# Selective attention and a routed feed-forward layer: the second expert unit's first layer as seven block products

## Chip, core and metric

The kernel runs on one core of a Trainium2 chip. The metric is the time of one execution in microseconds (us), as the device reports it. The engines are TensorE (PE in the profile, with its weight loads as PEld), VectorE (DVE), ScalarE (ACT), GpSimd (POOL) and SyncE (SP, whose queue issues most transfers).

## What is computed

Eight batches of 576 tokens pass an attention layer of 8 heads of 64, whose scores carry a bias from the cumulated `s`. Its output, 512 wide, goes into a feed-forward layer with 8 experts of width 1024, one expert for each token. All is 32-bit.

```python
# attention: x[b, s, :] = softmax(scores + min(bias, 0)) @ v, heads side by side
logits = einsum('bsd,de->bse', x, w_gate)
local_gate = sigmoid(einsum('bsd,de->bse', x, w_local))
for b in range(B):
    prev_e = -1
    for s in range(S):
        fresh_e = argmax(logits[b, s])
        e = fresh_e if s == 0 or local_gate[b, s] < 0.5 else prev_e
        prev_e = e
        p = softmax(logits[b, s])
        h = maximum(x[b, s] @ w1[e], 0)       # 512 -> 1024
        out[b, s] = p[e] * (h @ w2[e])        # 1024 -> 512
```

## The kernel before

The first 202 us are the attention. As batches become ready, the router reads off each token's expert ("codes"), ranks the tokens of an expert, and GpSimd stores their rows into a table in DRAM that is sorted by expert (`scatter`, L371). The last batch's codes and ranks come after the attention (`last_codes`, `late_rows`).

The experts then work through 17 units. A unit is a number of rows of one expert; the letters of `ORDER` say which kind: P and D are 256 rows, X is wider, M and T are made of smaller pieces. Which expert a unit has is only known at run time: `assign_early` places the first five units, `assign_doubles` the other whole units, and both are many tiny VectorE operations. They are generators; the three `yield`s of a whole-unit assignment are in `assign`.

A unit has two layers: phase (1, u) multiplies the turned rows xT by w1, with an activation (relu), phase (2, u) multiplies hT by w2. The phases go (1, 0), (1, 1), (2, 0), (1, 2), (2, 1), (1, 3), ... A layer is done in one of two ways:

- Plain (`layer1`): 8 groups of 4 products over 256 rows, each followed by a relu on ScalarE (L865, L867). A 32-bit product takes two passes through TensorE in the trace, so these are 64.
- Split (`layer_split`): the operands are cut into 2 x 2 blocks, a11 to a22 of the rows and b11 to b22 of the weights, and seven block products do for eight. They need sums of rows, s1 and s2 (`row_sums`, L704 to L706, and `row_fourth`, L710), and sums of weights, t1 and t2 and two in place (`weight_first` to `weight_fourth`, all recorded at L655). Product 6 takes s2 and t2, product 7 b12 after the third sum, product 4 b21 after the fourth. VectorE adds the products up (L763).

`SPLIT = ("DX", "PDX")` says which kinds are split: the first layer of D and X, the second of P, D and X. Sums of weights run on VectorE. Sums of rows run on VectorE in the first layers of the first five units (`adder`), else on GpSimd.

The engines work in the order in which the program issues their instructions. Within a phase, `at(i)` is called after each group or product, and runs what was put there: `plan(layer, unit, i, f)` and `job` (the same, with `i` held to the last step of that phase) hang functions to these places. At each step one pending store of table rows may go too (`self.puts`), held behind that step's ScalarE instruction, and further rows are fetched (`fetch`, L606, into xq, turned by `turn_x`, L641).

Of the kernel before, what the change touches and what calls it, by code (L numbers as in the profile page):

```python
# [63 lines left out]
WIDE, WIDE_MIN = DOUBLE + REST, DOUBLE + REST_MIN  # L64
EARLY = (4, 1)
PIECES = {"P": (DOUBLE,), "D": (DOUBLE,), "X": (WIDE,), "M": (HALF, HALF), "T": (HALF, QUARTER, QUARTER)}
ORDER = "PPDDDDDDDDXTXDMXD"
SPLIT = ("DX", "PDX")
LOOK, REST_FROM, REST_AT = 5, 8, (3, 4)
UNITS_OF = {size: sum(PIECES[u].count(size) for u in ORDER) for size in (DOUBLE, WIDE, HALF, QUARTER)}  # L70
SUM_MIN, SUM_MAX, ONE_MAX, END_MAX = 1e-19, 1e25, 1e12, 1e29
# [446 lines left out]
class Experts:  # L518
    def __init__(self, ctx, tc, w1, w2, out, table, router):
# [17 lines left out]
        loads = 0  # L537
        for kind in ORDER:
            at = []
# [354 lines left out]
    def run(self, recs, wend, out_of):  # L894
        tc, ctx, nc, router = self.tc, self.ctx, self.nc, self.router
# [71 lines left out]
        def plan(what, u, i, *fs):  # L967
            todo.setdefault((what, u, i), []).extend(fs)
# [2 lines left out]
        plan(1, 0, 2, last_codes)  # L971
        plan(1, 1, 1, lambda: loads(0))
        plan(1, 1, 2, late_rows)
        plan(1, 1, 5, lambda: list(router.assign_doubles()))
        rest = router.assign_rest()
        ranges = in_range(ctx, tc, recs, wend, router, out_of, self.bank, router.ones)
        plan(1, end - 1, 3, lambda: next(ranges))
# [10 lines left out]
        def job(what, u, i, f, *args):  # L988

            plan(what, u, i if i == "pre" else min(i, steps[self.kind(u)][what - 1] - 1), lambda: f(*args))  # L990

        for u in range(end):
            if u >= 2:
                job(2, u - 2, "pre" if u > 2 else 1, turn_x, u)
            for layer in range(2):
                if not self.split(u, layer):
                    continue
                if layer:
                    places = (2, u - 1, 5), (1, u + 1, "pre"), (1, u + 1, 2)
                    if u == 0:  # L1000
                        places = (1, 1, 6), (1, 1, 7), (1, 1, 7)
                    elif u == 1:
                        places = (2, 0, 5), (1, 2, 1), (1, 2, 3)
                    elif self.kind(u - 1) == "T":
                        places = (1, u + 1, 6), (1, u + 1, 6), (2, u, "pre")
                    place = (1, u + 1, int(self.deep(u) > 1)) if u + 1 < end else (2, u - 1, 0)
                    if u < 2:
                        place = ((1, 1, "pre"), (2, 0, 2))[u]
                    job(*place, self.row_sums, u, 1)
                else:  # L1010
                    places = (1, u - 1, 5), (2, u - 2, "pre"), (2, u - 2, 2)
                    if self.kind(u - 1) == "T":
                        places = (2, u - 2, 5), (2, u - 2, 6), (1, u, 0)
                    elif self.kind(u - 2) == "T":
                        places = ((2, u - 2, "pre"),) * 3
                    elif u == 2:
                        places = (2, 0, 4), (2, 0, 5), (1, 2, 0)
                    job(2, u - 2, 1 if self.kind(u - 2) in "DX" else "pre" if u > 2 else 3, self.row_sums, u, 0)
                for f, place in zip((self.weight_first, self.weight_second, self.weight_third), places):
                    job(*(place if place[1] < end else (2, u, "pre")), f, u, layer)  # L1020
            if self.kind(u) in "MT":
                for r, place in enumerate(((2, u - 1, 1), (2, u - 1, 3), (1, u + 1, 2), (1, u + 1, 3))):
                    job(*place, self.turn_h, u, r)
# [999 lines left out]
```

## Time and profile before

| | |
|---|---|
| three runs | 677.79, 679.24 (median), 680.12 us |
| profiled execution | 680.58 us, of it 678.8 in the span |
| TensorE, VectorE busy | 98%, 73% of the span |
| GpSimd, ScalarE busy | 54%, 29% of the span |
| granted clock of TensorE | 0.996 |
| unit 0 first layer begins | 202.5 us |
| unit 0 second layer begins | 232.2 us |

All times of the profile count from the start of the span, and the medians of the runs are of whole executions, so a sum over the span is to be put on the profiled execution's own time. A row of the timeline has the start in us, the time that the group of equal instructions took in us, the engine, the line, the operation, output<-inputs, shapes and how many; brackets at its end give the idle time of the engine just before it and what ended it. Tiles are named as in the program: w1b and w2b are weights, wt the sums t1 and t2 of them, xTs and hT the turned operands, xSs and hSs their sums, p the products in PSUM, sa and sb partial results.

### The profile page before, as it was taken

Reading aid. Unit: us, or ns where it says so; the run is one execution under the profiler, and the core shown is the slowest. Engines: PE = TensorE matmul, PEld = TensorE weight load, DVE = VectorE, ACT = ScalarE, POOL = GpSimd, SP = SyncE. Lnnn points to the kernel's source line nnn. Section 1 sums busy time; section 2 is a strip of 40 time slices with the busy share of each in tenths; the row PEclk is TensorE's granted clock in tenths of the full one; section 3 lists DMA queues with packets and bytes.
Section 4 is the critical chain, followed back from the end, with each engine's and each line's share of the span. In section 5 each row is a group of like instructions: output and inputs, shape, how many; then the busy total and the mean of one; then the engine's idle time right before and its main releaser. Section 6 shows DMA issues by size and latency. Waiting matters only on the chain.

```text
span 678.8 us, 18449 instructions
## 1 busy us (share of the span) xinstructions
PE 662.1 (98%) x7501; PEld 571.4 (84%) x7501; DVE 492.5 (73%) x942; ACT 195.3 (29%) x353; POOL 369.6 (54%) x525
## 2 busy tenths in 40 slices
PE   8999999999999999999999999999999999999995
PEld 7888877877788899999999999999589687796884
DVE  4665856886867799878988988955467664766843
ACT  4555635535522212212122122212211111111111
POOL 3562476776744888964555557540642542714733
PEclk9999999999999999999999999999999999999998
DMA  8665665766659798579977565616949796943002
GB/s 263 193 183 158 197 219 151 215 214 210 197 133 392 240 327 288 191 255 364 344 274 231 204 187 186 241 55 235 354 66 386 271 361 132 295 148 112 28 14 76
DMA packets 56549, 145.75 MB, mean 215 GB/s; under 512 B 13104, under 2 KB 33968, under 8 KB 51464
## 3 DMA queue, kind: packets, MB, share of 16 engines
q1 hardware_dynamic: 47352, 124.23, 55.8%
q0 software_dynamic: 9008, 20.11, 8.2%
q8 instruction: 61, 1.00, 0.6%
q14 instruction: 32, 0.26, 0.1%
q10 hardware_dynamic: 96, 0.15, 0.1%
HBM read 123.83 MB, written 20.85 MB: 213 GB/s over the span
## 4 chain that ended last, share of the span: by engine, by line
PE 86%; DVE 6%; issue 4%; POOL 2%; ACT 0%; POOLq 0%; DVEq 0%
PE p L731 26%; PE p L738 25%; PE ps L1218 11%; PE po L1275 6%; PE pb L1275 6%; PE hp L865 3%; PE yp L888 2%; PE hp L856 2%; PE lp L238 1%; PE ph L1236 1%; POOL out_dram L840 1%; DVE wt L655 1%; PE po L1288 1%; DVE w2b L655 1%; PE warm L1142 1%
## 5 line engine op out<-in xcount | busy, mean ns | idle before, releaser
L738 PE MATMUL p<-w2b,hT 128*128 128x256 f32 (+1 forms) x720 | 163.0, 379 | 0.0
L738 PEld LDWEIGHTS p<-w2b,hT 128*128 128x128 f32 (+1 forms) x720 | 133.3, 187 | 21.9 <-PE hp L856 1.6
L731 PE MATMUL p<-xTs,w1b 128*128 128x128 f32 (+1 forms) x1040 | 142.9, 295 | 0.0
L731 PEld LDWEIGHTS p<-xTs,w1b 128*128 128x128 f32 x1040 | 137.9, 191 | 3.6 <-issue 1.6
L1219 ACT ACTIVATE e<-ps 128x768 f32<-128x768 f32 (+1 forms) x96 | 76.4, 885 | 64.1 <-PE ps L1218 58.1
L840 POOL DMA_INDIRECT out_dram<-y,gi x37 | 46.9, 1269 | 74.2 <-ACT y L767 66.3
L767 ACT ACTIVATE y<-y,gi 128x256 f32<-128x256 f32 (+1 forms) x71 | 34.5, 505 | 161.6 <-DVE y L763 161.6
L771 ACT ACTIVATE hT<-hT 128x512 f32<-128x512 f32 (+1 forms) x52 | 36.8, 711 | 143.7 <-DVE hT L763 143.7
L1218 PE MATMUL ps<-qb,kb 64*128 64x384 f32 (+4 forms) x516 | 77.5, 446 | 0.2 <-ACT e L1219 0.2
L1218 PEld LDWEIGHTS ps<-qb,kb 64*128 64x128 f32 x516 | 47.7, 189 | 27.5 <-ACT e L1219 10.3
L371 POOL DMA_INDIRECT table<-xb,idx x54 | 57.3, 1062 | 15.8 <-issue 14.4
L738 PE MATMUL p<-wt,hSs 128*128 128x256 f32 (+1 forms) x272 | 63.3, 379 | 0.0
L710 POOL TENSOR_TENSOR hT<-hT,hSs 128x512 f32<-128x512 f32 (+1 forms) x14 | 21.1, 1508 | 76.8 <-PE p L738 76.8
L731 PE MATMUL p<-xSs,wt 128*128 128x128 f32 (+1 forms) x416 | 58.9, 295 | 0.5 <-DVE wt L655 0.5
L738 PEld LDWEIGHTS p<-wt,hSs 128*128 128x128 f32 (+1 forms) x272 | 50.7, 186 | 8.0
L1202 POOL TENSOR_SCALAR_AFFINE_SELECT e<-e 128x128 f32<-128x128 f32 (+1 forms) x96 | 35.7, 394 | 38.5 <-ACT e L1219 38.2
L731 PEld LDWEIGHTS p<-xSs,wt 128*128 128x128 f32 x416 | 55.6, 192 | 1.2 <-PE p L731 0.7
L763 DVE TENSOR_TENSOR hT<-p,sa 128x512 f32<-128x512 f32 (+1 forms) x48 | 31.2, 666 | 32.7 <-PE p L731 32.7
L1275 PE MATMUL pb<-vg,e 128*64 128x66 f32 x1280 | 41.9, 223 | 4.7 <-issue 4.7
L1275 PEld LDWEIGHTS pb<-vg,e 128*64 128x64 f32 x1280 | 39.7, 138 | 5.6 <-issue 5.4
L1275 PE MATMUL po<-vg,e 128*64 128x66 f32 x1280 | 41.6, 223 | 1.6 <-issue 1.6
L1275 PEld LDWEIGHTS po<-vg,e 128*64 128x64 f32 x1280 | 39.0, 138 | 3.2 <-issue 2.1
(304 smaller groups left out, 951.9 us busy)
## 6 DMA issues: line engine op xcount, KB each, us to landing
w2b<-in_w_dram SPq DMA_DIRECT2D x20, 2048.0 KB, 13.5
w1b<-in_w_dram SPq DMA_DIRECT2D x19, 2048.0 KB, 10.5
va<-in_v_dram SPq DMA_DIRECT2D x32, 320.0 KB, 3.4
xq<-table SPq DMA_DIRECT2D x72, 130.0 KB, 3.7
kb<-in_k_dram SPq DMA_DIRECT2D x31, 288.0 KB, 4.2
qb<-in_q_dram SPq DMA_DIRECT2D x31, 288.0 KB, 3.3
w1b<-in_w_dram SPq DMA_DIRECT2D x4, 512.0 KB
table<-xb,idx POOLq DMA_INDIRECT x54, 5.1
```

The source lines that it names most:

```text
L371: put = self.nc.gpsimd.indirect_dma_start(out=self.halves, in_=src, element_offset=0, in_offset=None, out_offset=bass.IndirectOffsetOnAxis ...
L710: self.adder(u, layer).tensor_tensor(a12, a12, (self.xS, self.hS)[layer][u][1], op=Alu.subtract)
L731: mm(ps[:, m * h : m * h + h], lhsT=b[:, k, (c * of + m) * P : (c * of + m) * P + P], rhs=a[:, k, :], start=m == 0 and k == 0, stop=m == o ...
L738: mm(ps[:p, c * w : c * w + w], lhsT=a[:, k, c * p : c * p + p], rhs=b[:, k, :], start=c == 0 and k == 0, stop=c == parts - 1 and k == n - 1)
L763: nc.vector.tensor_tensor(to[:, c], part, s[:, c], op=Alu.add)
L767: ins = nc.scalar.mul(to[:, c], to[:, c], gi[:p, parts * r + c, 1:2]).ins
L771: return gated(to, r) if layer else nc.scalar.activation(to, to, Act.Relu).ins
L840: put = nc.gpsimd.indirect_dma_start(out=out, out_offset=bass.IndirectOffsetOnAxis(ap=idx, axis=0), in_=y, element_offset=0, bounds_check= ...
L1202: nc.gpsimd.affine_select(out=ap, in_=ap, compare_op=Alu.is_ge, fill=0.0, base=base, pattern=n, channel_multiplier=-1)
L1218: mm(ps[:, h, at : at + z - a], lhsT=kb[d, key : key + P], rhs=qb[d, a:z], start=True, stop=True)
L1219: exps[n, u] = nc.scalar.activation(e[:, :, : WIDTH[u]], ps, Act.Exp, scale=scale).ins
L1275: of = mm(po[part][d, j - a, :], lhsT=weights_of(n, c, j, h), rhs=vgs[n % NV][:, c if j < 2 * G1 else G1 + c, h, :], start=(first and i == ...
```

## The change

Unit 1 becomes a D, so its first layer is split as well. Its row sums are put at step 3 of phase (1, 0), and its sums of weights at steps 4, 5 and 6, which is behind the last rows' codes on VectorE. The assignment of whole units, until now run in one go at step 5 of phase (1, 1), is taken up at five places, (1, 1, 5), (2, 0, 1), (2, 0, 3), (1, 2, 1) and (1, 2, 3); with three `yield`s it has four pieces, and the fifth call finds nothing left.

```diff
-ORDER = "PPDDDDDDDDXTXDMXD"
+ORDER = "PDDDDDDDDDXTXDMXD"
...
-        plan(1, 1, 5, lambda: list(router.assign_doubles()))
+        doubles = router.assign_doubles()
+        for place in ((1, 1, 5), (2, 0, 1), (2, 0, 3), (1, 2, 1), (1, 2, 3)):
+            plan(*place, lambda: next(doubles, None))
...
-                    job(2, u - 2, 1 if self.kind(u - 2) in "DX" else "pre" if u > 2 else 3, self.row_sums, u, 0)
+                    elif u == 1:
+                        places = (1, 0, 4), (1, 0, 5), (1, 0, 6)
+                    if u == 1:
+                        job(1, 0, 3, self.row_sums, u, 0)
+                    else:
+                        job(2, u - 2, 1 if self.kind(u - 2) in "DX" else "pre" if u > 2 else 3, self.row_sums, u, 0)
```

On VectorE, behind the last operation of the last rows' codes (L315), before the change come the last rows' ranks:

```order
L315 SCALAR_TENSOR_TENSOR incl<-seg,hot 128x152
L332 TENSOR_TENSOR at<-pos,base 128x144
L334 TENSOR_TENSOR base<-base,pos 128x8
L335 TENSOR_TENSOR at<-at,hot 128x144
L337 TENSOR_REDUCE row<-at 128x18
```

and after it unit 1's sums of rows and weights, with two additions behind its products:

```order
L315 SCALAR_TENSOR_TENSOR incl<-seg,hot 128x152
L704 TENSOR_TENSOR xSs<-xTs 128x256
L705 TENSOR_TENSOR xSs<-xSs,xTs 128x256
L706 TENSOR_TENSOR xTs<-xTs 128x2x128
L655 TENSOR_TENSOR wt_4100<-w1b 128x1024
L655 TENSOR_TENSOR wt_4100<-w1b,wt_4100 128x1024
L655 TENSOR_TENSOR w1b<-w1b 128x2x512
L763 TENSOR_TENSOR hT<-p_4167,sa 128x4x128
L655 TENSOR_TENSOR w1b<-w1b,wt_4100 128x2x512
L710 TENSOR_TENSOR xTs<-xTs,xSs 128x2x128
L763 TENSOR_TENSOR sb<-p_4187,sa 128x512
L332 TENSOR_TENSOR at<-pos,base 128x144
```

Ten operations now stand between the codes and the ranks, whose stores into the table wait for them.

On VectorE, before unit 0's sums of weights for its second layer (wt from w2b), the rest of the assignment stood in one piece:

```order
L413 TENSOR_SCALAR bof<-be 128x7
L416 TENSOR_SCALAR bstep<-n_f 128x8
L418 TENSOR_TENSOR bstep<-bstep,start 128x8
L419 TENSOR_TENSOR bstep<-bstep,start 128x7
L420 TENSOR_TENSOR bpast<-bpast,bstep 128x56
L423 TENSOR_REDUCE br<-bpast 128x7
L424 SCALAR_TENSOR_TENSOR br<-lane,br 128x7
L426 TENSOR_SCALAR bof<-br,start 128x7
L433 TENSOR_TENSOR bused<-n_f,bend 128x8
L434 TENSOR_SCALAR bused<-bused 128x8
L435 TENSOR_TENSOR bused<-bused,n_f 128x8
L466 TENSOR_TENSOR a0used<-a0used,bused 128x8
```

and now only its first piece does:

```order
L413 TENSOR_SCALAR bof<-be 128x7
L763 TENSOR_TENSOR hT<-p_4289,sb 128x4x128
L655 TENSOR_TENSOR wt_4300<-w2b 128x1024
L655 TENSOR_TENSOR wt_4300<-w2b,wt_4300 128x1024
L655 TENSOR_TENSOR w2b<-w2b 128x4x256
L763 TENSOR_TENSOR y<-p_4321,sa 128x256
L655 TENSOR_TENSOR w2b<-w2b,wt_4300 128x4x256
L416 TENSOR_SCALAR bstep<-n_f 128x8
```

The pieces from L416 and from L423 stand behind unit 0's sums now, and the one from L433 behind unit 2's second sum of weights.

On TensorE unit 1's 20 remaining plain products behind the ranks' (L323, L324) become four block products, with three ahead of them; before:

```order
L238 MATMUL lp<-xt_3689,wx 32x96 x32
L865 MATMUL hp<-xTs,w1b 128x256 x32
L323 MATMUL pos<-incl,first 128x152
L324 MATMUL pos<-hot,later 128x152
L865 MATMUL hp<-xTs,w1b 128x256 x20
```

and after:

```order
L865 MATMUL hp<-xTs,w1b 128x256 x20
L731 MATMUL p_4154<-xTs,w1b 128x128 x8
L731 MATMUL p_4167<-xTs,w1b 128x128 x8
L731 MATMUL p_4187<-xSs,wt_4100 128x128 x8
L323 MATMUL pos<-incl,first 128x152
L324 MATMUL pos<-hot,later 128x152
L731 MATMUL p_4226<-xTs,w1b 128x128 x8
L731 MATMUL p_4239<-xSs,wt_4100 128x128 x8
L731 MATMUL p_4253<-xTs,w1b 128x128 x8
L731 MATMUL p_4289<-xTs,w1b 128x128 x8
```

The third block product (p6, from xSs and wt) needs VectorE's sums, and the ranks' products stand behind it. In the other places that the text speaks of, GpSimd has one table store less in unit 1's first phase and one more behind, and unit 3's row sums move to step 1 of phase (2, 1), since unit 1 is now a D.

## The prediction

> **What bounds the kernel now.** I read the page first: the busy times of TensorE (PE) and VectorE (DVE), and the engines of the chain that ended last.
>
> ```profile
> PE 662.1 (98%) x7501; PEld 571.4 (84%) x7501; DVE 492.5 (73%) x942; ACT 195.3 (29%) x353; POOL 369.6 (54%) x525
> PE 86%; DVE 6%; issue 4%; POOL 2%; ACT 0%; POOLq 0%; DVEq 0%
> ```
>
> TensorE is nearly always busy and carries the chain, so a passage taken off it should shorten the kernel. But VectorE's 73% is an average. The busy times by stage, from the start of unit 1's first layer to the end of unit 1's second, say more (columns: stretch, its length, then busy us and instruction count of PE, weight loads, DVE, ACT, POOL, then granted clock, DMA share, GB/s):
>
> ```profile
> 217.86:223.97 6.11, 6.11 (x31) 5.45 (x30) 0.00 (x1) 1.54 (x4) 5.34 (x6) 1.00 0.74 286
> 223.97:232.67 8.70, 8.70 (x42) 7.65 (x41) 7.65 (x40) 1.61 (x5) 7.27 (x17) 1.00 0.81 198
> 232.67:244.30 11.63, 11.63 (x56) 10.23 (x55) 11.43 (x13) 1.19 (x3) 10.36 (x11) 1.00 1.00 391
> 244.30:248.57 4.27, 3.92 (x34) 3.70 (x32) 4.27 (x7) 1.02 (x2) 2.26 (x4) 1.00 0.69 195
> 248.57:271.70 23.13, 22.98 (x153) 21.49 (x154) 22.85 (x31) 5.66 (x11) 19.40 (x32) 1.00 0.86 291
> ```
>
> VectorE does nothing in the first stretch and is then nearly full for 47 us (what is missing in the second are the gaps between small operations that follow from one another), and in the fourth stretch TensorE is the one that pauses. The waits name that pause: the first layer of unit 2 waited for VectorE's second sum of weights.
>
> ```profile
> PE p L731 <- DVE wt L655: 0.5, 1, 0.5
> ```
>
> So after 224 us both engines are bounds at once. Now the timeline of weight loads, which shows TensorE's pace:
>
> ```profile
> 209.33 13.68 PEld L865 LDWEIGHTS hp<-xTs,w1b 128*128 128x128 f32 x64
> ...
> 223.64 8.52 PEld L865 LDWEIGHTS hp<-xTs,w1b 128*128 128x128 f32 x40
> 232.19 3.43 PEld L738 LDWEIGHTS p<-w2b,hT 128*128 128x128 f32 x16
> 235.64 1.70 PEld L738 LDWEIGHTS p<-wt,hSs 128*128 128x128 f32 x8
> ...
> 244.27 3.76 PEld L731 LDWEIGHTS p<-xTs,w1b 128*128 128x128 f32 x32
> 248.69 1.86 PEld L731 LDWEIGHTS p<-xSs,wt 128*128 128x128 f32 x16 [0.66 <-PE p L731]
> ...
> 269.60 3.76 PEld L731 LDWEIGHTS p<-xTs,w1b 128*128 128x128 f32 x32
> ...
> 282.21 3.33 PEld L738 LDWEIGHTS p<-w2b,hT 128*128 128x128 f32 x16
> ```
>
> **What TensorE gains.** A whole unit's plain first layer is 64 passes. Forty of them take 232.19 - 223.64 = 8.55 us, so 64 take 13.68; unit 1's begin at 209.33 + 40 x 0.2138 = 217.88. The same layer as seven products without a wait, unit 3's, lasts 282.21 - 269.60 = 12.61 us. The gain is 1.07 us, 0.16% of the span. A difference within 0.3%, 2.0 us, is about what a measurement of this kernel cannot tell from none, so this alone could not be seen.
>
> **What VectorE gets.** The work added is three row sums and the fourth (L704 to L706, L710), four sums of weights (L655) and seven additions behind the products (L763). Their rows in units 2 and 3:
>
> ```profile
> L655 DVE TENSOR_TENSOR wt<-w1b x3: 1212/1214/1214, 244.7 to 281.6; 128x1024 f32<-128x1024 f32 x3
> ...
> L655 DVE TENSOR_TENSOR w1b<-w1b,wt x3: 1214/1215/1877, 250.6 to 298.9; 128x1024 f32<-128x1024 f32 x3
> ```
>
> and, from the timeline:
>
> ```profile
> 251.75 0.42 DVE L710 TENSOR_TENSOR xTs<-xTs,xSs 128x256 f32<-128x256 f32 x1
> ...
> 256.35 1.28 DVE L763 TENSOR_TENSOR hT<-p,sa 128x512 f32<-128x512 f32 x2
> ...
> 260.55 0.42 DVE L704 TENSOR_TENSOR xSs<-xTs 128x256 f32<-128x256 f32 x1
> ...
> 261.35 0.42 DVE L706 TENSOR_TENSOR xTs<-xTs 128x256 f32<-128x256 f32 x1
> ```
>
> The lines of the first view are the first and last of the four sums of weights, by ns min/median/max: 1.21 us each by the median. The sum is 4 x 0.42 + 4 x 1.21 + 7 x 0.64 = 11.0 us; neighbours overlap a little (260.55 to 261.35 is 0.80 for two of 0.42), so I take 10.6. What it meets on VectorE:
>
> ```profile
> 217.25 0.47 DVE L315 TENSOR_TENSOR_SCAN incl<-seg,hot 128x152 f32<-128x152 f32 x1
> ...
> 223.97 0.31 DVE L332 TENSOR_TENSOR at<-pos,base 128x144 f32<-128x144 f32 x1 [6.24 <-PE pos L324]
> ...
> 227.28 0.16 DVE L388 TENSOR_TENSOR cnt<-base,base 128x8 int32<-128x8 f32 x1
> ...
> 230.41 0.16 DVE L416 TENSOR_SCALAR bstep<-n_f 128x8 f32<-128x8 f32 x1
> ...
> 231.85 0.28 DVE L433 TENSOR_TENSOR bused<-n_f,bend 128x8 f32<-128x8 f32 x1
> ...
> 232.67 1.22 DVE L655 TENSOR_TENSOR wt<-w2b 128x1024 f32<-128x1024 f32 x1
> 233.92 1.23 DVE L655 TENSOR_TENSOR wt<-w2b,wt 128x1024 f32<-128x1024 f32 x1
> ...
> 247.36 1.21 DVE L655 TENSOR_TENSOR wt<-w1b,wt 128x1024 f32<-128x1024 f32 x1
> ```
>
> The idle stretch before L332 holds 6.24 us of the 10.6. The rest pushes what follows: the last rows (3.3 us up to L388), the assignment (L388 to 232.67), unit 0's sums for its second layer. The assignment's last three pieces are now behind those sums, so 232.67 - 230.41 = 2.26 us of it goes out of their way. Unit 0's second-layer sums then start 10.6 - 6.24 - 2.26 = 2.1 us later, and the second of them is done at 235.15 + 2.1 = 237.25. TensorE, 1.07 us ahead, wants it at 235.64 - 1.07 = 234.57: a first wait of 2.7 us where there was none.
>
> By unit 2's second sum (done at 248.57 before) two of the three pieces have been paid back; only the last, 232.67 - 231.85 = 0.82 us, stands behind it. VectorE is then 10.6 - 6.24 - 0.82 = 3.5 us late, and TensorE, which already waited there, is 3.5 us late with it. The 1.07 us are inside that, not on top. Behind it unit 3's seven products run through in 12.61 us, so there the sums are early enough, and as the waits show only that one pause of TensorE for VectorE, nothing is left that could take the delay back: it reaches the end.
>
> **Collisions with GpSimd (POOL).** VectorE's idle 6 us were GpSimd's: it makes unit 0's row sums there. The first two rows are the first and last of three. What happens when both add from SBUF is seen in the others, from unit 0's second layer:
>
> ```profile
> 220.45 1.28 POOL L704 TENSOR_TENSOR hSs<-hT 128x512 f32<-128x512 f32 x1
> ...
> 223.03 1.27 POOL L706 TENSOR_TENSOR hT<-hT 128x512 f32<-128x512 f32 x1
> ...
> 236.54 4.19 DVE L655 TENSOR_TENSOR w2b<-w2b,wt 128x1024 f32<-128x1024 f32 x1
> ...
> 237.13 1.28 POOL L710 TENSOR_TENSOR hT<-hT,hSs 128x512 f32<-128x512 f32 x1
> ...
> 238.36 1.27 POOL L704 TENSOR_TENSOR hSs<-hT 128x512 f32<-128x512 f32 x1
> ...
> 239.71 2.15 POOL L705 TENSOR_TENSOR hSs<-hSs,hT 128x512 f32<-128x512 f32 x1
> ```
>
> The VectorE sum took 4.19 instead of 1.21 us: it stood still for two GpSimd operations, 2.55 us, and a little more. The added sums run from about 219 to 225 us and meet those three (1.28 + 1.27 and one between, 3.8 us together). Bounds: nothing, if they slip between, and all 3.8. I take two of three, 2.5 us, as in the row of 4.19. In unit 0's second layer four GpSimd operations collide before and after; I cost that difference at nothing, between -3.0 (4.19 back to 1.21) and nothing more.
>
> The Trainium skill, SBUF — State Buffer, "Who interferes with whom", says that a VectorE operation with two SBUF inputs and a GpSimd operation that reads SBUF exclude each other, and that whichever starts first keeps the ports. The trace agrees that one blocks the other, but here the VectorE sum started 0.59 us ahead and was the one that stood. By the rule all three operations would be paid in turn, 3.8 instead of 2.5, and the sum below would be 1.3 higher.
>
> **Moved and hidden.** ScalarE loses eight plain activations and gets a copy and four; it is idle most of the time in each stretch above. One store of unit 1's steps moves on, and GpSimd's stores of the last rows start up to 3.5 + 2.5 us later with their indices. Behind the last of them SyncE's queue holds the fetch of unit 5:
>
> ```profile
> 292.82 1.90 SPq L606 DMA_DIRECT2D xq<-table  x4
> ...
> 308.14 1.23 DVE L641 STREAM_TRANSPOSE xTs<-xq 128x1024 f32<-128x1024 f32 x1
> ```
>
> It has 13 us before VectorE turns it, and the turn moves back as well: nothing. Unit 1's weights were read by TensorE at 217.88 without a wait, so the sums at about 219 find them. The reload over them now waits for their fourth sum too, done before TensorE has finished with them: nothing. Unit 3's row sums move behind a sum of weights, which then comes earlier: nothing.
>
> **The sum.** 3.5 + 2.5 = 6.0 us later: span 684.8, and with the 1.8 us around it 686.6 for an execution like the profiled one (680.58). That one lies 1.3 us above the median of the three runs, 679.24, so I forecast 685.2.
>
> **Rivals.**
> - The collisions move away (not slower). Place: the fourth sum at 236.54. GpSimd's operations there come later, behind the late stores, and may fall on VectorE's small assignment steps: 3.0 us come back, and the first three may slip between. Then 3.5 - 3.0 = +0.5, 679.7. It decides where unit 2's second sum is at most 2 us after 248.57. For it: a small shift suffices. Against: VectorE has hardly a step there without two SBUF inputs. If VectorE lost nothing at all, TensorE's gain alone would give 678.2; only beyond that lies faster.
> - TensorE's clock falls in the pause. Its start, at the slow rate:
>
> ```profile
> 1.13 3.79 PE L1142 MATMUL warm<-xb 128*128 128x128 f32 x16 [1.13 <-DVE xb L1123]
> ```
>
> Sixteen passes take 3.79 us, against 3.76 for 32 at 269.60: half rate, 1.9 us lost. The pause at unit 0's p6, 2.7 us and up to 2.5 more, could bring this back: 6.0 + 1.9 = +7.9, 687.1. Against: the granted clock is 1.00 in all five stretches, but none has such a pause. The Trainium skill, TensorE: Matmul & The Clock Gate, "What's actually happening", puts the fall at about 3.4 us of idling; by it the pause is on the edge.
> - The late stores hold back SyncE: only if they slip by more than 13 us; then some 690.
>
> **How the numbers follow.** Forecast 0.60, clock 0.14, late stores 0.02: slower 0.76. Collisions gone or all hidden: same 0.21. Faster by over 0.3% needs a gain that I see nowhere: 0.03. The range goes from the first rival, 679.7, to 3.5 + 3.8 + 1.9 = +9.2, 688.4.
>
> **What the profile after would show.** Right: no idle time of VectorE before L332; a sum of weights of unit 1 stretched beyond 2 us beside GpSimd's L704 to L706; TensorE waiting for VectorE's L655 at p6 of unit 0's second layer and again at unit 2's, 5 to 7 us in all; unit 1's first layer 12.6 us plus its own wait. Wrong: TensorE without those waits; unit 2's first layer starting before 245; VectorE idle between 225 and 250.

## The result and the profile after

| | before | after |
|---|---|---|
| median of the runs (4 each) | 679.43 us | 688.01 us |
| profiled execution; its span | 680.58; 678.8 us | 688.45; 686.7 us |
| start of unit 0's first layer | 202.5 us | 203.5 us |
| from there to the end of the span | 476.3 us | 483.2 us |

The changed kernel takes 1.0117 times as long, 95% interval 1.0098 to 1.0136: 8.6 us slower by the medians. Of the 7.9 us between the two spans 6.9 lie behind the start of unit 0's first layer. The rest is the attention, which the change doesn't touch. Over the profiles of this study, but for the last three, its end lay between 201.7 and 206.3 us, so below I compare the stretch behind it, from the start of unit 0's first layer to the end of the span ("from unit 0"). It comes from the one profile of each version. Its last part, from unit 4's first layer on, took 384.6 to 385.1 us in the first ten profiles, so differences of half a microsecond mean nothing there; larger ones are traced to rows below.

The page of the changed kernel first: busy times of TensorE and VectorE, and the engines of the chain that ended last.

```profile
PE 664.1 (97%) x7549; PEld 573.7 (84%) x7549; DVE 503.8 (73%) x957; ACT 195.2 (28%) x350; POOL 372.4 (54%) x525
PE 79%; POOL 7%; issue 5%; DVE 4%; DMA 2%; ACT 1%; SPq 0%; POOLq 0%; DVEq 0%
```

TensorE has lost seven points of the chain, most of them to GpSimd and DMA. What GpSimd has gained lies between 265 and 300 us, and the last section of the experiments comes back to it. What TensorE waited for, from the view of waits (us in total, times, longest):

```profile
PE p L738 <- DVE wt L655: 5.0, 1, 5.0
PE p L738 <- POOL gap L839: 0.9, 1, 0.9
```

Before, the only such row was 0.5 us for unit 2. Now the rows of TensorE's weight loads around the first wait:

```profile
222.49 1.87 PEld L731 LDWEIGHTS p<-xSs,wt 128*128 128x128 f32 x16
...
231.94 3.33 PEld L738 LDWEIGHTS p<-w2b,hT 128*128 128x128 f32 x16
240.62 3.06 PEld L738 LDWEIGHTS p<-wt,hSs 128*128 128x128 f32 x8 [5.36 <-issue]
243.77 2.11 PEld L738 LDWEIGHTS p<-w2b,hT 128*128 128x128 f32 x8
245.91 1.70 PEld L738 LDWEIGHTS p<-wt,hSs 128*128 128x128 f32 x8
...
255.11 1.86 PEld L731 LDWEIGHTS p<-xSs,wt 128*128 128x128 f32 x16 [0.26 <-PE p L731]
```

Unit 1's p6 (222.49) finds its sums, so the seven products run through, and unit 0's second layer starts 28.5 us after unit 0's first instead of 29.7. Its p6 (240.62) then stands for 5.0 us and runs on at nearly half rate: 3.06 and 2.11 us for eight passes that take 1.70, at a granted clock of 0.50 and 0.81. When TensorE comes to unit 2's p6 (255.11) it stands for only 0.26 us: the delay was paid at the pause and in the slow passes, and TensorE and VectorE arrive there almost together. The busy times by stage (stretch, length, busy us and count of PE, weight loads, DVE, ACT, POOL, granted clock, DMA share, GB/s) have the clock of that stretch, 0.82, and VectorE full in the first stretch, where it did nothing before:

```profile
218.82:224.50 5.68, 5.68 (x51) 5.65 (x50) 5.61 (x7) 0.97 (x2) 5.09 (x5) 1.00 0.72 277
...
231.94:251.09 19.15, 14.17 (x58) 11.87 (x57) 18.29 (x41) 2.63 (x5) 12.30 (x16) 0.82 0.86 306
```

VectorE's rows show why TensorE stands:

```profile
220.98 1.23 DVE L655 TENSOR_TENSOR wt<-w1b,wt 128x1024 f32<-128x1024 f32 x1
222.12 2.29 DVE L655 TENSOR_TENSOR w1b<-w1b 128x1024 f32<-128x1024 f32 x1
224.94 1.69 DVE L655 TENSOR_TENSOR w1b<-w1b,wt 128x1024 f32<-128x1024 f32 x1
226.55 1.49 DVE L710 TENSOR_TENSOR xTs<-xTs,xSs 128x256 f32<-128x256 f32 x1
228.56 0.29 DVE L332 TENSOR_TENSOR at<-pos,base 128x144 f32<-128x144 f32 x1
...
239.28 1.23 DVE L655 TENSOR_TENSOR wt<-w2b,wt 128x1024 f32<-128x1024 f32 x1
...
241.89 1.21 DVE L655 TENSOR_TENSOR w2b<-w2b,wt 128x1024 f32<-128x1024 f32 x1
243.03 1.23 DVE L416 TENSOR_SCALAR bstep<-n_f 128x8 f32<-128x8 f32 x1
244.29 1.19 DVE L418 TENSOR_TENSOR bstep<-bstep,start 128x8 f32<-128x8 f32 x1
...
245.71 1.17 DVE L420 TENSOR_TENSOR bpast<-bpast,bstep 128x56 f32<-128x56 f32 x1
...
253.78 1.21 DVE L655 TENSOR_TENSOR wt<-w1b,wt 128x1024 f32<-128x1024 f32 x1
```

The idle time before L332 is gone; three of unit 1's sums are stretched to 2.29, 1.69 and 1.49 us. Unit 0's second sum (239.28) ends 37.05 us after unit 0's start, 4.4 later than before; unit 2's (253.78) 51.53 after it, 5.46 later. The fourth sum, 4.19 us before, takes 1.21, but three assignment steps, on tiles of 128x8 and 128x56, take 1.2 us each. GpSimd's rows beside them:

```profile
221.82 1.51 POOL L704 TENSOR_TENSOR hSs<-hT 128x512 f32<-128x512 f32 x1
223.41 2.14 POOL L705 TENSOR_TENSOR hSs<-hSs,hT 128x512 f32<-128x512 f32 x1
225.51 2.24 POOL L706 TENSOR_TENSOR hT<-hT 128x512 f32<-128x512 f32 x1
...
242.63 1.60 POOL L710 TENSOR_TENSOR hT<-hT,hSs 128x512 f32<-128x512 f32 x1
244.19 1.26 POOL L704 TENSOR_TENSOR hSs<-hT 128x512 f32<-128x512 f32 x1
```

The first three meet unit 1's sums, and both sides are stretched; L710 begins 0.5 us before the fourth sum ends and leaves it at its usual length; it and the sums behind it meet the small steps instead.

### The profile page after: what moved, and what is told of

The parts are those of the page before. It is cut to its first block, busy times and chain, and to the rows that moved or that the text cites. A ratio compares the mean times of both kernels' runs of the same rounds, so it can differ in the third digit from the quotient of the medians.

```text
span 686.7 us, 18560 instructions
## 1 busy us (share of the span) xinstructions
PE 664.1 (97%) x7549; PEld 573.7 (84%) x7549; DVE 503.8 (73%) x957; ACT 195.2 (28%) x350; POOL 372.4 (54%) x525
## 4 chain that ended last, share of the span: by engine, by line
PE 79%; POOL 7%; issue 5%; DVE 4%; DMA 2%; ACT 1%; SPq 0%; POOLq 0%; DVEq 0%
PE p L731 24%; PE p L738 21%; PE ps L1225 11%; PE po L1282 6%; PE pb L1282 6%; POOL table L371 3%; PE hp L865 2%; PE yp L888 2%; PE hp L856 2%; DMA w1b<-in_w_dram 2%; POOL out_dram L840 2%; PE lp L238 1%; PE ph L1243 1%; DVE wt L655 1%; PE po L1295 1%
## 5 line engine op out<-in xcount | busy, mean ns | idle before, releaser
L731 PE MATMUL p<-xTs,w1b 128*128 128x128 f32 (+1 forms) x1120 | 152.3, 293 | 0.0
L731 PEld LDWEIGHTS p<-xTs,w1b 128*128 128x128 f32 x1120 | 147.2, 192 | 3.6 <-issue 1.6
L771 ACT ACTIVATE hT<-hT 128x512 f32<-128x512 f32 (+1 forms) x56 | 39.3, 705 | 160.0 <-DVE hT L763 160.0
L738 PE MATMUL p<-wt,hSs 128*128 128x256 f32 (+1 forms) x272 | 65.1, 387 | 5.0 <-DVE wt L655 5.0
L710 POOL TENSOR_TENSOR hT<-hT,hSs 128x512 f32<-128x512 f32 (+1 forms) x14 | 21.4, 1530 | 76.8 <-PE p L738 76.7
L731 PE MATMUL p<-xSs,wt 128*128 128x128 f32 (+1 forms) x448 | 62.8, 293 | 0.1
L731 PEld LDWEIGHTS p<-xSs,wt 128*128 128x128 f32 x448 | 59.3, 192 | 0.8 <-PE p L731 0.3
L763 DVE TENSOR_TENSOR hT<-p,sa 128x512 f32<-128x512 f32 (+1 forms) x51 | 33.2, 668 | 32.5 <-PE p L731 32.5
```

Source lines behind the costliest of these rows:

```text
L710: self.adder(u, layer).tensor_tensor(a12, a12, (self.xS, self.hS)[layer][u][1], op=Alu.subtract)
L731: mm(ps[:, m * h : m * h + h], lhsT=b[:, k, (c * of + m) * P : (c * of + m) * P + P], rhs=a[:, k, :], start=m == 0 and k == 0, stop=m == o ...
L738: mm(ps[:p, c * w : c * w + w], lhsT=a[:, k, c * p : c * p + p], rhs=b[:, k, :], start=c == 0 and k == 0, stop=c == parts - 1 and k == n - 1)
L763: nc.vector.tensor_tensor(to[:, c], part, s[:, c], op=Alu.add)
L771: return gated(to, r) if layer else nc.scalar.activation(to, to, Act.Relu).ins
```

## Experiments

Every ratio is to runs of the kernel before that were timed beside the experiment, with the 95% interval in brackets.

### The sums, the additions, and both

Three runs leave out the four sums of weights of unit 1's first layer, its seven additions, or both. The assignment's pieces stay at their five places.

Without the sums:

```diff
     def weight_first(self, u, layer):      # second, third, fourth: return
+        if (u, layer) == (1, 0):
+            self.wT[u, layer] = [b12, b22]
+            return
```

> The change without unit 1's four sums of weights in the first layer; the plain blocks b12 and b22 stand in for t1 and t2, so the products are as many and as long. Theory V: VectorE gets back 4 x 1.2 us and most of the 2.6 us that these and the fourth row sum lost to GpSimd, some 6 to 7 us: no pause at unit 0's sixth product, none at unit 2's, no fall of the clock, and the gain of the seven products shows: -1.1 us, some 678.3. Rival S (the split itself costs, through the products' order, the banks or the later stores): still 2 us or more slower than before, 681.5 or more.

Measured: ratio 1.0053 (1.0025 to 1.0081); from unit 0 479.9 us. I had expected no wait at all, and TensorE still waits 1.5 us at p6 of unit 0 and 2.0 at unit 2; by the number rival S was right. VectorE's row before unit 1's first addition tells why:

```profile
224.49 0.69 DVE L772 TENSOR_TENSOR hT<-p,sa 128x512 f32<-128x512 f32 x1 [3.10 <-PE p L740]
```

It idles again, since an addition can't start before its product. The idle time that the prediction had counted for all of the added work takes sums, and of the seven additions only the two that stand ahead of the ranks; the other five stand behind them.

Without the additions:

```diff
+        bare = (u, layer) == (1, 0)
...
+                if bare:
+                    if to is not s2 and to is not s3:
+                        bare_relu(to[:, c], part)
+                    continue
...
```

> The changed kernel, with the seven additions behind the block products of unit 1's first layer left out: ScalarE takes the products straight out of PSUM, so unit 1's rows are wrong and nothing else. The sums of rows and weights stay. Theory V2 (VectorE's idle stretch ahead of the last rows can take in sums of weights, which have their inputs early, but not the additions, which wait for TensorE's products; the additions are what makes unit 2's second sum late): VectorE comes 4 to 5 us sooner to unit 0's second-layer sums, TensorE's pause at p6 there falls from 5.0 to at most 1 us, and unit 2's second layer starts 80 to 82 us after unit 0's first (85.17 changed, 79.71 before): 3 to 5 us less than the changed kernel, about 684 us. Rival theory W (the sums of weights and GpSimd's collisions with them carry the loss): the pause stays above 3 us and no more than 1.5 us come back.

Measured: 1.0047 (1.0022 to 1.0071); 480.0 us. The pause at p6 of unit 0 falls to 1.3 us (V2: at most 1, W: above 3), and 3.2 us come back (V2: 3 to 5, W: at most 1.5). So V2 is nearer, but unit 2's second layer starts 83.2 us after unit 0's first, and V2 had 80 to 82. What is left shows in the waits at unit 2 (first row) and at unit 0's p6 (second row):

```profile
PE p L731 <- DVE wt L655: 2.1, 1, 2.1
PE p L738 <- DVE wt L655: 1.3, 1, 1.3
```

Without both:

> The changed kernel, with both the four sums of weights and the seven additions of unit 1's first layer left out (the blocks b12 and b22 stand in for the sums, ScalarE reads the products from PSUM), so unit 1's rows are wrong. Only the row sums are left of VectorE's added work. Theory V2: TensorE's gain of 1.07 us shows at last. TensorE waits nowhere for VectorE by more than 0.7 us, and the time from the start of unit 0's first layer to the end of the span is 475 to 476 us (476.3 before, 483.2 changed). Measured against before: 0 to 1.3 us less, some 679. Rival theory S (the split as such costs: its order of products, its PSUM banks or the late stores): at least 2 us of the 6.9 stay although VectorE has nothing to do for it.

The edits are those of the two runs above. Measured: 1.0038 (1.0012 to 1.0065); 479.0 us, where V2 had 475 to 476. With none of the change's added VectorE work left but the sums of rows, and the assignment's pieces at the new places, TensorE still waits at unit 2, 3.1 us, and behind it runs at half rate (granted clock 0.51; 16 passes take 1.87 otherwise):

```profile
253.72 3.37 PEld L740 LDWEIGHTS p<-xSs,wt 128*128 128x128 f32 x16 [3.21 <-issue]
```

So V2 was not the whole, and S was right that something stays. The versions compare best on the way, counted from the start of unit 0's first layer to the end of VectorE's second sum for unit 0's second layer, and to the start of unit 2's p6:

| | unit 0's second sum done | unit 2's p6 begins | from unit 0 |
|---|---|---|---|
| before | 32.65 us | 46.19 us | 476.3 us |
| neither sums nor additions | 30.58 | 47.44 | 479.0 |
| additions alone | 33.56 | 48.16 | 479.9 |
| sums alone | 33.42 | 48.03 | 480.0 |
| both, the changed kernel | 37.05 | 51.65 | 483.2 |

At unit 0's second sum the two add up: 3.0 and 2.8 us alone, 6.5 together. At unit 2's p6 each alone costs only 0.6 to 0.7, and both cost 4.2. The run with neither loses there what it had gained: it idles 0.61 us for a product of TensorE, and its fourth sum meets GpSimd and takes 3.68 us, where the other three versions of the split, later at that point, take 1.2. The last column mixes in two effects behind unit 2's p6. TensorE's fallen clock costs 1.5 us in the version with neither and 1.6 with the sums alone, and a wait for GpSimd, below, 1.2 us with the additions alone and in the changed kernel. The 2.7 us that stay with neither are 1.25 of lateness and 1.5 of the clock.

### The assignment's pieces

The pieces alone, in the kernel before:

```diff
-        plan(1, 1, 5, lambda: list(router.assign_doubles()))
+        doubles = router.assign_doubles()
+        for place in ((1, 1, 5), (2, 0, 1), (2, 0, 3), (1, 2, 1), (1, 2, 3)):
+            plan(*place, lambda: next(doubles, None))
```

> The kernel before, with the assignment of whole units in its four pieces at the five places; unit 1's first layer stays plain. By the prediction's terms VectorE starts unit 0's second-layer sums 2.3 us sooner and unit 2's second sum 0.8 us sooner, so that TensorE's 0.5 us wait there goes: 475.6 to 475.8 us from unit 0's first layer to the end of the span (476.3 before), 0.7 us at most, which no timing here can tell from none. Rival: the pieces, moved beside GpSimd's row sums, take 1.2 us for each small step as they do in the changed kernel, and VectorE loses 3 us there; then unit 2's wait grows to 2 us or more and the kernel is 1.5 to 2.5 us slower.

Measured: 1.0062 (1.0038 to 1.0085); 479.8 us, 3.5 more than before, with not one operation added. The rival came true, and for more than its reason: two small steps take 1.2 us, and about as much again is lost as idle time. VectorE:

```profile
232.62 1.22 DVE L655 TENSOR_TENSOR w2b<-w2b 128x1024 f32<-128x1024 f32 x1
236.12 0.42 DVE L763 TENSOR_TENSOR y<-p,sa 128x256 f32<-128x256 f32 x1 [2.29 <-PE p L738]
236.46 3.61 DVE L655 TENSOR_TENSOR w2b<-w2b,wt 128x1024 f32<-128x1024 f32 x1
240.00 1.23 DVE L416 TENSOR_SCALAR bstep<-n_f 128x8 f32<-128x8 f32 x1
241.27 1.19 DVE L418 TENSOR_TENSOR bstep<-bstep,start 128x8 f32<-128x8 f32 x1
...
249.88 1.21 DVE L655 TENSOR_TENSOR wt<-w1b,wt 128x1024 f32<-128x1024 f32 x1
```

Before, VectorE came to the row of 236.12 without idling. Now it is 2.4 us early there and waits 2.29 for TensorE's product. The time taken out ahead of that point is lost as idle time, the fourth sum meets GpSimd as before, and the moved steps stand behind it, in front of unit 2's second sum (249.88 instead of 247.36). TensorE waits 3.0 us there, and 0.7 more for unit 1's fourth sum.

This is also what stayed without sums and additions. From the start of the addition that TensorE releases (236.12 here) to the end of unit 2's second sum VectorE takes 14.97 us here, 15.00 in that run and 12.37 in the kernel before. That run was only 1.3 us earlier at the addition, since TensorE was 1.2 us ahead. So S's reasons, the order of products and the banks, are not needed for what stayed.

All of it in one piece again, in the changed kernel:

```diff
-        for place in ((1, 1, 5), (2, 0, 1), (2, 0, 3), (1, 2, 1), (1, 2, 3)):
-            plan(*place, lambda: next(doubles, None))
+        plan(1, 1, 5, lambda: list(router.assign_doubles()))
```

> The change with the assignment of whole units in one go again, at step 5 of phase (1, 1); unit 1 stays split. Theory V (VectorE is the bound from 224 us to unit 2's sixth product, and its total work sets the time): the 2.26 us of the last three pieces go back in front of unit 0's second-layer sums, so TensorE's pause there grows from 5.0 to about 7.3 us, but by unit 2's second sum only 0.82 us more stand ahead; as the small steps no longer meet GpSimd's row sums there (three of them took 1.2 us each in the changed kernel instead of 0.2), up to 3 us less. Time between 2 us below and 1 us above the changed kernel: 686 to 689 us. Rival C (what costs is TensorE's pause and the half clock behind it): the pause grows by 2.3, so the time does: 690.

Measured: 1.013 (1.0097 to 1.0162); 484.6 us. The pause at unit 0's p6 grows to 7.2 us, as the theory had it, and the small steps take 0.17 to 0.33 us each. But the theory let at most 0.82 us of that reach unit 2. Unit 2's p6 comes 2.4 us later than in the changed kernel, and TensorE doesn't wait there; VectorE now waits for TensorE:

```profile
249.58 0.42 DVE L763 TENSOR_TENSOR sa<-p,sb 128x256 f32<-128x256 f32 x1 [1.97 <-PE p L738]
```

Here the pause and the slow passes behind it set the time at unit 2, as rival C said (2.3). Of the 2.4 us 1.4 are left at the end, because this version doesn't have the 1.2 us wait for GpSimd treated below. So the five places that cost 3.5 us in the kernel before save 1.4 to 2.4 in this one. By the ratios alone the two versions aren't told apart.

Three runs look for a place that costs nothing. They were timed beside runs of the kernel before with a median of 687.45 us, 6.6 or more above the others, and no profile of the kernel before was taken among these. So their ratios are the measure; the times from unit 0 are given beside the expected ones. The pieces behind unit 2's second sum, in the kernel before:

```diff
+        for place in ((1, 2, 3), (1, 2, 4), (1, 2, 5), (1, 2, 6)):
+            plan(*place, lambda: next(doubles, None))
```

> The kernel before, with the assignment of whole units in its four pieces at steps 3 to 6 of phase (1, 2), behind unit 2's second sum of weights; unit 1's first layer stays plain. Theory V3 (what counts is the work between two fixed points on VectorE: the fourth sum of unit 0's second layer, which a product of TensorE releases, and unit 2's second sum; work taken away ahead of the first point only makes VectorE idle there, work put between the two delays TensorE): VectorE idles some 5 us ahead of the fourth sum, nothing more stands between the points, TensorE's wait of 0.5 us at unit 2 goes, and 475.6 us are left from the start of unit 0's first layer to the end of the span (476.3 before, 479.8 with the pieces at the five places). Rival: the pieces cost wherever they stand beside GpSimd's stores: again 2 us or more above before.

Measured: 1.0103 (1.0082 to 1.0125), from unit 0 485.8 us (475.6 expected): against V3. Its VectorE:

```profile
242.68 0.42 DVE L763 TENSOR_TENSOR y<-p,sa 128x256 f32<-128x256 f32 x1 [6.28 <-ACT sa L785]
243.02 1.22 DVE L655 TENSOR_TENSOR w2b<-w2b,wt 128x1024 f32<-128x1024 f32 x1
...
246.17 1.72 DVE L704 TENSOR_TENSOR xSs<-xTs 128x256 f32<-128x256 f32 x1
247.93 1.37 DVE L705 TENSOR_TENSOR xSs<-xSs,xTs 128x256 f32<-128x256 f32 x1
249.22 1.49 DVE L706 TENSOR_TENSOR xTs<-xTs 128x256 f32<-128x256 f32 x1
...
276.58 1.21 DVE L655 TENSOR_TENSOR w2b<-w2b,wt 128x1024 f32<-128x1024 f32 x1
```

As said, 6.28 us are idle ahead of the fourth sum. But the collision only moves: the fourth sum is short now, and unit 2's row sums take 4.5 us instead of 1.5, so TensorE still waits 1.6 us for unit 2's second sum. And the pieces now stand ahead of unit 1's fourth sum (276.58), for which TensorE waits 4.9 us. The last two of unit 1's products then run at half rate, 6.26 us instead of 3.43. V3 was right on the points at which TensorE releases VectorE, and wrong that there are no others behind.

The same in the changed kernel, with the edit of the stores' run below:

> The changed kernel, with the assignment's four pieces at steps 3 to 6 of phase (1, 2) instead of the five places, and the fourth sum of rows of unit 2's second layer on VectorE; nothing is left out. From the changed kernel's rows: 2.8 us of small steps (L388 to L413) leave the way of unit 0's sums, so TensorE's pause at p6 there falls from 5.0 to 2.1 us; behind the fourth sum 3.8 and 0.6 us of small steps go, so that unit 2's second sum comes 44.3 us after the start of unit 0's first layer and TensorE, which wants it at 46.3, doesn't wait. Theory V3: 476.3 + 2.1 - 1.1 - 0.7 = 476.6 us to the end of the span, about the time before; up to 3 more where the fourth sum meets GpSimd again. Rival (the split layer costs by itself): 480 or more.

Measured: 1.0098 (1.0066 to 1.013), from unit 0 484.6 us (476.6 expected). The pause at unit 0's p6 is 2.3 us (2.1 expected) and unit 2 doesn't wait, but unit 1's fourth sum is 3.2 us late. Beside the changed kernel's 1.0117 no difference is shown. And with the last rows' ranks behind unit 0's third sum:

```diff
-        plan(1, 1, 2, late_rows)
+        plan(1, 1, 6, late_rows)      # behind unit 0's sums of weights
...
```

The three conditions that wait for the last rows' stores go by the new place too.

> As the run with late pieces and the fourth sum on VectorE, and with the last rows' ranks (L332 to L382, 3.3 us on VectorE) behind unit 0's third sum of weights for its second layer; nothing is left out. Theory V3: nothing of the change now stands ahead of unit 0's second sum but the additions, TensorE's pause at p6 is 0 to 0.5 us; the ranks lie in VectorE's wait for the product ahead of the fourth sum, of which at most 0.5 us reach TensorE; the gain of the seven products shows: 474 to 475 us from unit 0's first layer to the end of the span, 1.3 to 2.3 less than before. Rival: the stores of the last rows, now some 8 us later than in the changed kernel, hold back GpSimd's sums of rows or unit 5's rows, and TensorE waits 1 to 5 us for them.

Measured: 1.0185 (1.0161 to 1.0209), from unit 0 491.0 us (474 to 475 expected), the slowest of all. Neither theory has it: VectorE waits in the additions of unit 1's first layer (a row of 5.21 us idle, put down to TensorE's next layer), and TensorE waits three times for VectorE, 4.0, 2.6 and 3.6 us. What holds that addition is open.

### GpSimd's row sums

Unit 0's second layer without its three sums of rows on GpSimd, in the changed kernel:

```diff
     def row_sums(...):
+        if (u, layer) == (0, 1):
+            of[u] = self.rows_of(t, u)[1]
+            return
```

> The change without the three GpSimd operations that make unit 0's row sums for its second layer (3.8 us when undisturbed); the plain blocks a21 and a22 stand in. Theory V with the collisions as a term of its own: unit 1's sums take 1.2 us each again, VectorE is 2.6 us earlier; TensorE's pause at unit 0's sixth product is about 2.4 us, the clock does not fall, unit 2's sixth product starts 2 to 2.6 us earlier; 685.5 to 686. Rival K (VectorE loses nothing to GpSimd that it would not lose elsewhere): within 0.7 us of the changed kernel, 687.5 or more.

Measured: 1.0067 (1.0041 to 1.0092); 481.2 us, 2.0 less than the changed kernel. Unit 1's sums take 1.22 us each again, and the pause at p6 falls from 5.0 to 2.4. So these collisions cost 2.6 us at that point, and unit 2's p6 starts 2.6 us sooner. Behind it the clock, which falls after a wait of 2.1 us at unit 2, takes 1.6 us back, and the wait for GpSimd of the section on the stores is missing, which gives 1.2.

### The clock

The changed kernel with 18 products of identities in the pause at unit 0's p6, into a bank that nobody reads:

```diff
+        if (u, layer) == (0, 1):
+            fill = self.bank("fill")
+            for _ in range(18):
+                self.nc.tensor.matmul(fill[:, :P], lhsT=self.router.ident, rhs=self.router.ident, start=True, stop=True)
```

> The change with 18 products of the identity with itself (36 passes, about 4.0 us) in TensorE's 5.0 us pause ahead of unit 0's sixth product, into a bank that nobody reads. The pause is then too short for the clock to fall; the sixth product takes 1.7 us in the weight loads again instead of 3.1, the seventh 1.7 instead of 2.1. Theory V: VectorE is as late as before at unit 2's second sum, so TensorE waits there about 1.8 us instead of 0.3, and the time stays within 0.5 us of the changed kernel: 688. Rival C (the clock's fall is part of the loss): 1.8 us less, 686.2.

Measured: 1.0118 (1.0094 to 1.0141); 483.5 us, as the changed kernel. The passes behind the pause are at full rate:

```profile
242.89 1.59 PEld L738 LDWEIGHTS p<-wt,hSs 128*128 128x128 f32 x8 [1.12 <-issue]
...
257.37 1.86 PEld L731 LDWEIGHTS p<-xSs,wt 128*128 128x128 f32 x16 [2.21 <-issue]
```

Unit 2's first layer then starts 1.95 us sooner and waits 2.0 us for VectorE's second sum. The fall of the clock is real, 1.8 us, and costs nothing in the changed kernel, because VectorE decides when unit 2 goes on. Where TensorE itself is the later one behind the pause it does cost: the falls at unit 2's p6 in the runs above reach the end with 1.5 to 1.6 us.

### The stores in front of GpSimd's fourth sum

Behind unit 2 the changed kernel loses 1.16 us more: from the start of unit 2's second layer to unit 4's first it takes 13.15 us, 11.99 before. The rows of weight loads at its two ends, and those of TensorE and of GpSimd near its end:

```profile
288.63 3.33 PEld L738 LDWEIGHTS p<-w2b,hT 128*128 128x128 f32 x16
...
301.78 3.76 PEld L731 LDWEIGHTS p<-xTs,w1b 128*128 128x128 f32 x32
```

```profile
300.17 1.99 PE L738 MATMUL p<-w2b,hT 128*128 128x256 f32 x8 [0.90 <-POOL gap L839]
```

```profile
297.85 0.96 POOL L371 DMA_INDIRECT table<-pad,pad_i  x1 [0.22 <-issue]
298.83 1.28 POOL L710 TENSOR_TENSOR hT<-hT,hSs 128x512 f32<-128x512 f32 x1
```

The product waits for L710, and L710 stands behind the table's last stores. In the kernel before, that layer begins at 282.21 and unit 4's first layer with this row:

```profile
294.20 3.76 PEld L731 LDWEIGHTS p<-xTs,w1b 128*128 128x128 f32 x32
```

The changed kernel with this one sum on VectorE:

```diff
-        self.adder(u, layer).tensor_tensor(a12, a12, ..., op=Alu.subtract)
+        on = self.nc.vector if (u, layer) == (2, 1) else self.adder(u, layer)
+        on.tensor_tensor(a12, a12, ..., op=Alu.subtract)
```

> The changed kernel, with the fourth sum of rows of unit 2's second layer on VectorE instead of GpSimd; nothing is left out. Theory Q (the late stores of the last rows stand in front of that sum on GpSimd, and TensorE's third product waits for it): phase (2, 2) lasts 11.99 us again instead of 13.15, TensorE's wait for GpSimd is gone, and the time from unit 0's first layer to the end of the span falls by 1.2 us from 483.2 to 482.0. Rival (the 1.16 us are the weights' or the rows' transfers that come late there): the phase stays at 13.1 us, and another wait is named.

Measured: the phase takes 11.98 us and the wait for GpSimd is gone; from unit 0 482.3 us, 1.0 less; ratio 1.0076 (1.0046 to 1.0107). On VectorE the sum takes 0.68 us and finds its place:

```profile
293.72 0.68 DVE L711 TENSOR_TENSOR hT<-hT,hSs 128x512 f32<-128x512 f32 x1
```

So Q holds in that L710 waits in GpSimd's queue. That the stores are late is not shown to be the reason: the run without sums of weights has the ranks at nearly the old time (L332 starts 21.74 us after unit 0's first layer, 21.47 before, 25.10 in the changed kernel) and the same wait. What it shares with the changed kernel is a seventh store between GpSimd's third sum of rows and L710, where the kernel before has six. The versions with one piece, without row sums, without additions and without both have seven too and no wait, so the count alone doesn't decide either; no run tested it by itself. By the ratios alone this kernel isn't told apart from the changed one. None of these versions beats the kernel before.

## Why the prediction held, point by point

It gave 685.2 us, 679.7 to 688.4; the median is 688.01, near the upper end, and slower, as forecast. The 8.6 us against a forecast of 6.0 are 5.46 us of VectorE's lateness, 1.16 for GpSimd's sum, 0.3 in the rest of the units, and the remainder from the attention and between executions.

- **TensorE's gain.** Right: 1.07 expected, 1.2 measured (29.7 to 28.5), without a wait of unit 1's p6, and nothing of it reached the end.
- **The idle time of VectorE.** Filled, as forecast. That it takes 6.24 us of any added work was wrong: the run without sums of weights idles 3.1 us there.
- **First collisions.** 2.5 us expected; 1.08 + 0.48 + 1.07 = 2.6 measured on three sums, and 2.6 at the pause in the run without row sums. By the rule of the Trainium skill, SBUF — State Buffer, "Who interferes with whom", as the prediction read it, it would have been 3.8. The rows look like engines taking turns: GpSimd's three were stretched too, to 1.51, 2.14 and 2.24 us from 1.28 and 1.27. So the size came out by the choice of two of three; the picture behind it, one sum that stands still for two whole GpSimd operations, did not.
- **Unit 0's second sum and the pause.** 2.1 + 2.5 = 4.6 us late expected, 4.4 measured; a pause of 2.7 + 2.5 = 5.2 expected, 5.0 measured. The second wait that the prediction named as a sign, at unit 2, was only 0.26 us: the pause and the slow passes had already made TensorE as late as VectorE.
- **Unit 2's second sum.** 6.0 us late expected, 5.46 measured, but through two errors that cancel, which is luck. The prediction costed the change in the collisions of unit 0's second layer at nothing: the fourth sum gave its 3.0 us back, as the first rival said, and L416, L418 and L420 took them again, 1.23 + 1.19 + 1.17 us instead of 0.33 + 0.17 + 0.22 in the run with one piece.
- **What the pieces are worth.** The prediction took 2.26 us out of the sums' way as a gain at full value. In the kernel before they are worth nothing there, since VectorE then waits for a product, and cost 3.5 us behind it. In the changed kernel, where VectorE never idles in that stretch, the subtraction holds at the pause, 5.0 us against 7.2 with one piece. But for unit 2 the prediction counted a gain of 0.82 us, and it was 2.4 there, 1.4 at the end.
- **The clock as a rival.** It fell, for 1.8 us against the rival's 1.9, but they lie beside VectorE's lateness: the run that kept the clock up gained nothing. The rival's 687.1 lies nearer to the result than the forecast, for a wrong reason.
- **Late stores.** "Nothing" was wrong by 1.16 us. I had followed them to SyncE's queue and to the fetch of unit 5, not along GpSimd's own, where a sum that TensorE needs stands behind them. The store of unit 1's steps that "moves on" was costed at nothing too, and the wait comes with a seventh store in front of that sum; whether it is that store or the lateness stays open.

## What to carry to other kernels

Add up work on a busy engine only between two points where another engine releases it: what is taken out ahead of such a point turns into idle time, and what is put behind it counts in full. Idle time takes work whose inputs lie ready, not work that waits for the engine that is to be relieved. A late step is to be followed along its own engine's queue first: the next instruction behind it may be one that the bounding engine waits for. And compare versions at the point where they part, not only at the end: here a slower clock and another queue moved the end by more than the terms in question.

## What the runs showed of the chip

- A VectorE step on 128x8 numbers took 1.2 us instead of 0.17 to 0.33 beside GpSimd's row sums, in the changed kernel and in seven of the experiments: each can lose about as much to one GpSimd operation as a large sum does, so that three of them lost what the fourth sum had gained.
- TensorE's clock fell behind pauses of different lengths. It fell after 5.0 and 7.2 us (granted clock 0.50), after 3.1 us (0.51) in the run without sums and additions, and after 2.1 us (0.65) in the run without additions, here:

```profile
250.15 2.78 PEld L731 LDWEIGHTS p<-xSs,wt 128*128 128x128 f32 x16 [2.22 <-issue]
```

It did not fall after 3.0 us (1.00) in the run with the pieces alone, here:

```profile
251.20 1.86 PEld L731 LDWEIGHTS p<-xSs,wt 128*128 128x128 f32 x16 [3.18 <-issue]
```

The run without GpSimd's row sums has both in one execution: not after 2.4 us (1.00), but 14 us later after 2.1 us (0.68). So no length of a pause decides it between 2.1 and 3.0 us. The Trainium skill, TensorE: Matmul & The Clock Gate, "What's actually happening", says that activity is counted in windows of 3.4 us that run freely; that would let the place of a pause in its window decide, but no run here shows the windows.
